# Pseudo-inverse steps, W and landmark scores on full 128x128 tiles of the multiplier, from batch 2 with block-diagonal operands

## The chip, the cores and the metric

The kernel runs on one core of one Trainium2 chip. The metric is the device time of one execution in microseconds (us); less is better. The matrix engine (PE) multiplies; VectorE (DVE), ScalarE (ACT) and GpSimd (POOL) work on elements; SyncE (SP) issues the transfers. PE can be used whole, as one array of 128x128, or as several smaller tiles that multiply side by side; the profile names the tile in each row (`128*128`, `128*64`, `32*32`: rows by columns).

## The reference, cut to what matters

Two stages for 8 batches of 576 positions: an approximate attention with 8 heads of 64 channels and 32 landmarks, then a layer with a Fourier transform and two large products. The attention:

```python
def _attn_ref(q, k, v):                       # (8, 8, 576, 64) each
    m, scale = 32, 1.0 / np.sqrt(D)
    q_lm = q.reshape(B, H, m, S // m, D).mean(axis=3)
    k_lm = k.reshape(B, H, m, S // m, D).mean(axis=3)
    A, Bm, C = sm(q, k_lm), sm(q_lm, k_lm), sm(q_lm, k)      # softmaxes
    Z = Bm.transpose(0, 1, 3, 2) / (norm1(Bm) * norminf(Bm) + 1e-06)
    for _ in range(6):
        Z = 2 * Z - Z @ Bm @ Z                # pseudo-inverse, 32x32 a head
    return A @ Z @ C @ v
def _moe_ref(x, w_ch1, w_ch2):                # x: (8, 576, 512)
    u = x + real(fft(fft(x, axis=1), axis=2))
    un = (u - mean(u)) / sqrt(var(u) + 1e-06)
    return u + relu(un @ w_ch1) @ w_ch2       # 512 to 2048 and back
```

## The kernel before, in words

**The order of the work.** Nothing is issued as the code runs. Each operation is recorded with its engine, a cost from a formula and what it reads and writes (`Order.op`, line 195; `Kernel.mm`, line 517, for multiplications). `Order.solve` (line 235) then plays the whole program with these costs and writes one fixed order for each engine: among what is ready it takes the lowest phase, and within a phase what has the longest chain behind it. Buffers come from pools (`SLOTS`, `BANKS`): four PSUM banks named `at` serve the attention, and from chunk 4 on two of these four are held for good by the second stage; `row` has six slots. On the chip, each engine runs its list strictly in that order. So a changed cost or a new operation can change the order on every engine. All instructions carry the line of the one place that emits them (L1307), so the rows are told apart by their tiles' names.

**The second stage** runs in 18 chunks of 256 positions. Each chunk multiplies by both weight matrices in three float16 products for each float32 one (`mm3`), with whole tiles: `hp<-unT,w` for the first matrix, `acc<-w,h`, `acc<-big,h`, `at<-big,h` and `at<-w,h` for the second. From chunk 4 (`SEVEN`) the second product is done in seven part products in place of eight, with sums made on DVE, ACT and POOL (`seven`).

**The attention** of the next batches is laid between these chunks. `attention` (line 658) loads q and k, makes the landmarks, and calls `landmarks` (line 923), which does the 32x32 work of all eight heads at once: heads are in two groups g of four, and the four 32x32 blocks of a group lie below each other on the 128 partitions. In order:

- landmark scores (lines 930 to 935): four multiplications `at<-lm,qbd` with 128x64 tiles, then a softmax to `Bd` and `nrm`.
- `BT` times its own transpose (lines 971 to 976): eight multiplications, one for each 32x32 block, `at<-BT` with 32x32 tiles.
- the values' product: `values` (batches 0 and 1) or `values_turned` (line 903, batches from `LATE` = 2 on) makes `R`, the product of the key softmax with v. In `values_turned` the 576 keys of a head go in four chunks of 128 keys and one of 64; the 64 left of two heads share the halves of one chunk, so this chunk is done in 64x32 tiles (first the low half, last the high half) and the others in 128x32 tiles. `load_v` (line 646) brings those 64 rows to both halves with two transfers.
- six pseudo-inverse steps (lines 982 to 995). `ES` holds the power E and the product S side by side, 64 columns for each group. A step multiplies each 32x32 block of E with its block of `ES`: eight multiplications `at<-nrm` or `at<-ES` in 32x32 tiles; the last one does only 32 columns. Then ACT copies E to the new `ES` and DVE adds to S.
- `nbd` (line 996): the result times a mask, as block-diagonal operands for what follows.
- W (lines 1002 to 1023): `at<-row,R` for the norm (two multiplications, 128x64 tiles) and `at<-R,row` (eight, 128x64 tiles).

A float32 multiplication is one instruction in the program and shows as two in the trace, each with a weight load; I call these passes.

Of the kernel before, what the change touches and what calls it, by code (L numbers as in the profile page):

```python
# [60 lines left out]
def tables():  # L61

    freqs = _tiles[0] + _tiles[1] + REST
    t1 = np.zeros((P, 4, 2, 160), np.float16)
    for i, (fn, o) in enumerate(((np.cos, 1), (np.sin, 0), (np.sin, 1), (np.cos, 0))):
        t1[:, i] = trig(fn, _tiles[0], freqs[o::2], S)
    t1t = np.zeros((P, 2, 2, 320), np.float16)
    t2 = np.zeros((P, 4, 2, 2, NC), np.float16)
    there = [f is not None for f in FREQS]
    for x, fn in enumerate((np.cos, np.sin)):  # L70
        t1t[:, x] = trig(fn, REST * 2, freqs[0::2] + freqs[1::2], S)
        for g in range(2):
# [4 lines left out]
    mask = np.zeros((P, 6), np.float32)  # L77
    mask[:, 0:4] = p[:, None] // 32 == np.arange(4)
    mask[:, 4:6] = p[:, None] // 64 == np.arange(2)
    diag = (p[:, None] % 32 == np.arange(32)).astype(np.float32)  # L80
    return t1, t1t, t2, diag, mask
# [5 lines left out]
KEEP = ("at", "row")  # L87
# [81 lines left out]
class Op:  # L169
    __slots__ = ("engine", "calls", "held", "took", "phase", "group", "margin", "seq", "before", "after", "tiles", "claims", "rank", "start", "end", "nbytes", "port", "name", "other", "urgent")  # L170


class Order:
# [21 lines left out]
    def op(self, engine, held, took, writes, reads, call, nbytes=0, port=False):  # L195
        o = self.bundle if engine == "PE" and self.bundle else None
        if o is None:
            o = Op()
            o.engine, o.calls, o.held, o.took, o.seq = engine, [], 0.0, 0.0, len(self.ops)
            o.phase, o.group, o.margin, o.nbytes, o.port = self.phase, self.group, self.margin, nbytes, port  # L200
            o.other, o.urgent = {}, False
            o.before, o.after, o.tiles, o.claims, o.name = dict.fromkeys(self.gate), [], {}, self.claims, ""
            self.claims = []
            self.ops.append(o)
            if engine == "PE" and self.bundle is not None:
                self.bundle = o
        o.calls.append(call)
        o.held += held
        o.took = o.held + took
        for v in reads:  # L210
            self.touch(o, v, False)
        for v in writes:
            self.touch(o, v, True)

# [20 lines left out]
    def solve(self):  # L235
# [11 lines left out]
        pipe, port, now, done = 0.0, 0.0, 0.0, []  # L247
# [58 lines left out]
        while events:  # L306
# [22 lines left out]
            for e in [e for e in best if e not in again] + again:  # L329
# [17 lines left out]
                o.start = now  # L347
                free[e] = now + o.held
# [72 lines left out]
class Kernel:  # L421
    def __init__(self, ctx, tc, NB, q, k, v, w1, w2, t1, t1t, t2, diag, mask, out):
# [20 lines left out]
        self.mask = self.const(mask, [P, 6], F32, "mask")  # L443
        self.mask4, self.mask2 = self.mask[:, 0:4], self.mask[:, 4:6]
# [72 lines left out]
    def mm(self, out, a, b, start=True, stop=True, share=1.0):  # L517
        n, m = math.prod(b.shape[1:]), math.prod(a.shape[1:])
        if a.dtype != F32:
            held = max(0.02, 0.003 + n / 2400 * share + (0.01 if share < 1.0 or 100 < n < 200 else 0.0))  # L520
        else:
            held = max(0.2, 0.02 + 4 * n / 2400) * (m / 128 if m < 128 else 1.0) * share
        self.order.op(
            "PE", held * self.cold, 0.2, [out], [a, b],
            (self.nc.tensor, "matmul", (out, a, b), {"start": start, "stop": stop, "skip_group_check": True}),
        )
        self.order.ops[-1].name = "mm"

    def tr(self, out, a, ident):
        self.order.op("PE", 0.21 * self.cold, 0.2, [out], [a, ident], (self.nc.tensor, "transpose", (out, a, ident), {}))  # L530
        self.order.ops[-1].name = "tr"

# [113 lines left out]
    def load_v(self, b, loads):  # L646
        for g in range(2):
# [182 lines left out]
    def values(self, loads, Cs, ci, R):  # L830
        V, A, mm, tr = self.V, self.A, self.mm, self.tr
        for g in range(2):
# [20 lines left out]
            V.tensor_scalar(R[:, g], ps[:, 0:64], Cs[g][1], ci[:, g : g + 1], ALU.mult, ALU.mult)  # L853
# [49 lines left out]
    def values_turned(self, loads, T, ci, R):  # L903
# [5 lines left out]
        low, high = slice(0, 64), slice(64, P)  # L909
        for g in range(2):  # L910
# [10 lines left out]
            V.tensor_scalar(R[:, g], ps[:, 0:64], ci[:, g : g + 1], 2.0**-14, ALU.mult, ALU.mult)  # L921

    def landmarks(self, b, loads, qbd, lm):
# [5 lines left out]
        R = small([P, 2, 64], "R")  # L929
# [6 lines left out]
        V.tensor_scalar(Bd.rearrange("p g m -> p (g m)"), ps[:, 0:64], 1.0 / 2592.0, None, ALU.mult)  # L936
# [33 lines left out]
        blocks = [slice(32 * i, 32 * i + 32) for i in range(4)]  # L970
        pse = self.at()
        self.together()
        for g in range(2):
            for i in blocks:
                mm(pse[i, 32 * g : 32 * g + 32], BT[i, g], BT[i, g])
        self.apart()
# [4 lines left out]
        ES = nrm[:, :, 0:2].rearrange("p g x m -> p g (x m)")  # L981
        for it in range(6):
            c0 = 0 if it < 5 else 32
            ps = self.at()
            self.together()
            for g in range(2):
                for i in blocks:
                    mm(ps[i, 64 * g + c0 : 64 * g + 64], ES[i, g, 0:32], ES[i, g, c0:])
            self.apart()
            pv = ps[:, 0:128].rearrange("p (g m) -> p g m", g=2)  # L990
            new = small([P, 2, 64], "ES", bufs=3)
            if it < 5:
                A.copy(new[:, :, 0:32], pv[:, :, 0:32])
            V.tensor_tensor(new[:, :, 32:64], ES[:, :, 32:64], pv[:, :, 32:64], ALU.add)
            ES = new
        nbd = self.row(512).rearrange("p (g i m) -> p g i m", g=2, i=4)
        for g in range(2):
            self.E.tensor_tensor(
                nbd[:, g].rearrange("p i (d m) -> p i d m", d=2), ES[:, g, 32:].unsqueeze(1).unsqueeze(1).broadcast_to([P, 4, 2, 32]),
                self.mask4.unsqueeze(2).unsqueeze(3).broadcast_to([P, 4, 2, 32]), ALU.mult,  # L1000
# [3 lines left out]
        for g in range(2):  # L1004
            mm(pst[64 * g : 64 * g + 64, 0:128], R[:, g], nbd[:, g, :, 0:32])
# [29 lines left out]
        def rest():  # L1035
            WC = [self.mid().bitcast(F16)[:, 0 : 4 * NC].rearrange("p (y x t) -> p y x t", y=2, x=2) for g in range(2)]
            for x in range(2):
# [3 lines left out]
                for ya, yb in ((0, 0), (0, 1), (1, 0)):  # L1041
                    for i in range(4):
                        at = 32 * (2 * (i % 2) + i // 2)
                        for g in range(2):
                            rows = slice(64 * g, 64 * g + 64)
                            mm(pss[g][at : at + 32, 0:NC], Wt[rows, ya, i], self.t2[rows, i, yb, x], yb == 0 and ya == 0, ya == 1, 0.125)
# [328 lines left out]
```

## Time and profile before

| what | value |
|---|---|
| median of 3 runs | 965.61 us (965.14 to 967.0) |
| the profiled execution's own time | 965.58 us |
| its span in the profile | 963.4 us |
| busy PE, PE weight loads | 911.0, 731.0 us |
| busy DVE, ACT, POOL | 760.1, 482.8, 216.5 us |
| PE instructions | 10510 |

The span is 2.2 us shorter than the execution's own time. In a group's row stand the line, the engine, the operation, the tiles written and read (buffer numbers left out), the shapes, the count, then the busy time in us and the mean of one in ns. In a timeline's row the first number is the start in us from the beginning of the span, the second the time from the first start to the last end of the merged instructions. Matmuls are pipelined: one that lasts 0.27 us in the profile can follow the one before after 0.11 us, so what a stretch costs PE is read from start to start.

### The profile page before, as it was taken

Reading aid. Unit: us, or ns where it says so; the run is one execution under the profiler, and the core shown is the slowest. Engines: PE = TensorE matmul, PEld = TensorE weight load, DVE = VectorE, ACT = ScalarE, POOL = GpSimd, SP = SyncE. Lnnn points to the kernel's source line nnn. Section 1 sums busy time; section 2 is a strip of 40 time slices with the busy share of each in tenths; the row PEclk is TensorE's granted clock in tenths of the full one; section 3 lists DMA queues with packets and bytes.
Section 4 is the critical chain, followed back from the end, with each engine's and each line's share of the span. In section 5 each row is a group of like instructions: output and inputs, shape, how many; then the busy total and the mean of one; then the engine's idle time right before and its main releaser. Section 6 shows DMA issues by size and latency. Waiting matters only on the chain. (4 is left out here: it accounts for less than half of the span.)

```text
span 963.4 us, 26055 instructions
## 1 busy us (share of the span) xinstructions
PE 911.0 (95%) x10510; PEld 731.0 (76%) x10510; DVE 760.1 (79%) x2016; ACT 482.8 (50%) x1007; POOL 216.5 (22%) x250
## 2 busy tenths in 40 slices
PE   5767999999999999999999999999999999999997
PEld 3546667666666788888887778887888878888886
DVE  7989996898898769887789886996698858665455
ACT  5999842355455445454454444545345533333332
POOL 0211210153643213321223002242031303101010
PEclk9768999999999999999999999999999999999999
DMA  9966110734737433556252733467235522435231
GB/s 350 355 226 178 41 37 13 182 105 95 258 90 189 157 89 104 155 124 213 67 155 88 195 104 89 133 130 216 67 100 154 132 74 73 120 112 117 82 105 50
DMA packets 161993, 128.23 MB, mean 133 GB/s; under 512 B 80080, under 2 KB 150736, under 8 KB 161744
## 3 DMA queue, kind: packets, MB, share of 16 engines
q1 hardware_dynamic: 161872, 126.57, 45.3%
q8 instruction: 82, 1.34, 0.6%
q14 instruction: 39, 0.32, 0.1%
HBM read 94.15 MB, written 14.68 MB: 113 GB/s over the span
## 5 line engine op out<-in xcount | busy, mean ns | idle before, releaser
L1307 PE MATMUL hp<-unT,w 128*128 128x256 f16 x3264 | 388.5, 273 | 10.3 <-DMA unT<-row 8.9
L1307 PEld LDWEIGHTS <-w 128*128 128x128 f16 (+1 forms) x3584 | 345.0, 99 | 68.5 <-issue 10.4
L1307 PEld LDWEIGHTS <-h 128*128 128x128 f16 x2604 | 247.2, 98 | 61.9 <-issue 6.6
L1307 PE MATMUL acc<-w,h 128*128 128x256 f16 (+1 forms) x1260 | 198.6, 294 | 1.1 <-DVE u L1307 0.4
L1307 DVE TENSOR_TENSOR sum<-ws 128x256 f32<-128x256 f32 (+1 forms) x278 | 99.8, 405 | 69.9 <-ACT ws L1307 68.1
L1307 ACT ACTIVATE ws<-hp 128x512 f32<-128x512 f32 x112 | 66.6, 595 | 140.1 <-PE hp L1307 139.9
L1307 ACT CAST h<-sum 128x640 f16<-128x640 f32 x112 | 81.1, 724 | 82.6 <-DVE sum L1307 68.1
L1307 PE MATMUL at<-big,h 128*128 128x256 f16 x672 | 110.1, 273 | 0.0
L1307 POOL TENSOR_TENSOR sum<-ws 128x256 f32<-128x256 f32 (+1 forms) x58 | 41.3, 727 | 252.9 <-ACT ws L1307 197.9
L1307 DVE TENSOR_TENSOR h<-sum,h 128x640 f16<-128x640 f32 x79 | 65.0, 823 | 19.2 <-ACT h L1307 18.0
L1307 POOL TENSOR_TENSOR h<-sum,h 128x640 f16<-128x640 f32 x33 | 46.4, 1405 | 150.3 <-ACT h L1307 150.3
L1307 ACT CAST row<-row 128x256 f16<-128x256 f32 (+1 forms) x76 | 36.7, 505 | 40.4 <-DVE row L1307 32.2
L1307 DVE TENSOR_REDUCE lm<-big 128x32 f32<-128x576 f32 (+1 forms) x48 | 44.3, 946 | 14.7 <-DMA big<-k_dram 8.1
L1307 PE MATMUL at<-w,h 128*128 128x256 f16 x336 | 55.0, 273 | 0.0
L1307 PE MATMUL acc<-big,h 128*128 128x256 f16 x336 | 55.0, 273 | 0.0
L1307 PEld LDWEIGHTS <-big 128*128 128x128 f16 (+1 forms) x768 | 40.8, 104 | 11.0 <-issue 5.0
L1307 ACT CAST h<-ws 128x256 f16<-128x256 f32 x112 | 45.3, 404 | 2.7
L1307 DVE SCALAR_TENSOR_TENSOR u<-at,scw,row 128x128 f32<-128x128 f32 (+3 forms) x120 | 39.0, 386 | 3.7 <-PE at L1307 3.5
L1307 DVE TENSOR_TENSOR h<-ws,h 128x256 f16<-128x256 f32 x95 | 40.5, 426 | 0.0
L1307 ACT ACTIVATE big<-big 128x1168 f16<-128x1168 f32 (+1 forms) x26 | 25.3, 983 | 29.2 <-DMA big<-q_dram 21.7
L1307 PEld LDWEIGHTS <-mt 64*128 64x128 f16 (+1 forms) x752 | 28.6, 98 | 14.5 <-issue 8.0
L1307 DVE SCALAR_TENSOR_TENSOR u<-acc,winv,u 128x512 f32<-128x512 f32 x50 | 35.3, 741 | 3.0 <-PE acc L1307 2.7
(223 smaller groups left out, 1254.7 us busy)
## 6 DMA issues: line engine op xcount, KB each, us to landing
big<-sums SPq DMA_DIRECT2D x336, 128.0 KB, 2.2
w<-w_dram SPq DMA_DIRECT2D x22, 512.0 KB, 8.1
big<-q_dram SPq DMA_DIRECT2D x16, 584.0 KB, 6.2
big<-k_dram SPq DMA_DIRECT2D x16, 576.0 KB, 4.8
out_dram<-u SPq DMA_DIRECT2D x36, 256.0 KB, 2.2
big<-v_dram SPq DMA_DIRECT2D x12, 512.0 KB, 4.8
big<-w_dram SPq DMA_DIRECT2D x10, 512.0 KB, 6.5
sums<-row SPq DMA_DIRECT2D x40, 128.0 KB, 2.5
```

The lines of the kernel that those rows point to most:

```text
L1307: getattr(engine, name)(*map(real, args), **{k: real(x) for k, x in kw.items()})
```

## The change

**Block-diagonal operands.** From batch 2 on, the product of `BT` and the six steps use whole 128x128 tiles: the left operand of each group is spread to a block-diagonal 128x128 matrix in a `row` buffer (the 32 columns times a mask, four times beside each other), and one multiplication for each group replaces four. For the product of `BT` and the first step the spreading is given to DVE or POOL, as the planner decides; in the five following steps it reads the PSUM result and so is DVE's. ACT's copy stays.

**W and scores**, in all batches: `R` becomes a kept buffer `Rz` of [128, 2, 128] whose other half is zero (cleared once by POOL), so that `at<-Rz,row` is two multiplications with 128 columns that add into one bank; the eight of `at<-R,row` become four with 128 columns each; the order of heads in `nbd` and `Wt` goes along. The landmark scores are two multiplications with 128 columns in place of four with 64; half of their result isn't used, and two DVE operations take the other half in place of one.

**The values' product**, from batch 2: the fifth chunk is multiplied whole, with zero rows of v standing against the other head's keys, all in 128x32 tiles; 20 multiplications a group as before. `load_v` brings that chunk with three transfers in place of two.

**The planner's costs**: the least cost of a whole float32 multiplication goes from 0.2 to 0.13 us, and each change of the tile shape between multiplications costs 0.12 us (`SWITCH`).

```diff
-        self.mask = self.const(mask, [P, 6], F32, "mask")
+        self.mask = self.const(mask, [P, 10], F32, "mask")
+        self.Rz = self.kept([P, 2, P], F32, "Rz")
+        self.G.memset(self.Rz, 0.0)
...
-            held = max(0.2, 0.02 + 4 * n / 2400) * (m / 128 if m < 128 else 1.0) * share
+            held = max(0.032, max(0.13, 0.02 + 4 * n / 2400) * (m / 128 if m < 128 else 1.0) * share)
...
+                if o.modes:
+                    if o.modes[0] != mode:
+                        o.held += SWITCH
+                        o.took += SWITCH
+                    mode = o.modes[-1]
...
-                for x in range(2):
-                    self.dma(to[64 * x : 64 * x + 64, 4], src[0:64, 4])
+                of = lambda t, x: t[:, 4].rearrange("p (r x d) -> p r x d", r=2, x=2)[:, :, x]
+                self.dma(of(to, 0), of(src, 0))
+                for half in range(2):
+                    self.dma(of(to, 1)[64 * half : 64 * half + 64], of(src, 1)[64 - 64 * half : 128 - 64 * half])
...
-            tiles = [(0, low, 4, 4)] + [(x, slice(0, P), 5 * x + c, c) for c in range(4) for x in range(2)] + [(1, high, 4, 4)]
-            for x, rows, blk, c in tiles:
-                for r in range(2):
-                    i, at = 2 * r + x, 64 * g + 32 * r
-                    mm(ps[32 * i : 32 * i + 32, 0:64], E[rows, blk, at : at + 32], vf[rows, c, 64 * i : 64 * i + 64],
-                       (x, c) in ((0, 4), (1, 0)), (x, c) in ((0, 3), (1, 4)))
+            for c in range(5):
+                for i in range(4):
+                    at = 64 * g + 32 * (i // 2)
+                    blk = c if c == 4 else 5 * (i % 2) + c
+                    mm(ps[32 * i : 32 * i + 32, 0:64], E[:, blk, at : at + 32], vf[:, c, 64 * i : 64 * i + 64], c == 0, c == 4)
...
-            for pr in range(2):
-                mm(ps[64 * pr : 64 * pr + 64, 32 * g : 32 * g + 32], qbd[:, 2 * g + pr], lm[:, g, 64 + 32 * pr : 96 + 32 * pr])
+            mm(ps[:, 64 * g : 64 * g + 64], flat(qbd[:, 2 * g : 2 * g + 2]), lm[:, g, 64:128])
...
+        full = b >= LATE
+        def diagonal(src, E):
+            t = self.row(256).rearrange("p (g i m) -> p g i m", g=2, i=4)
+            for g in range(2):
+                E.tensor_tensor(
+                    t[:, g], src(g).unsqueeze(1).broadcast_to([P, 4, 32]), self.mask4.unsqueeze(2).broadcast_to([P, 4, 32]), ALU.mult
+                )
+            return t
+        def blockwise(ps, lhs, rhs, n, c0=0):
...
+                if full:
+                    mm(ps[:, out], lhs[:, g].rearrange("p i m -> p (i m)"), rhs[:, g, c0:])
+                else:
+                    for i in blocks:
+                        mm(ps[i, out], lhs[i, g], rhs[i, g, c0:])
...
+        lhs = diagonal(lambda g: nrm[:, g, 0], self.E) if full else ES[:, :, 0:32]
         for it in range(6):
...
-                for i in blocks:
-                    mm(ps[i, 64 * g + c0 : 64 * g + 64], ES[i, g, 0:32], ES[i, g, c0:])
+            blockwise(ps, lhs, ES, 64, c0)
             if it < 5:
                 A.copy(new[:, :, 0:32], pv[:, :, 0:32])
+                lhs = diagonal(lambda g: pv[:, g, 0:32], V) if full else new[:, :, 0:32]
...
-            mm(pst[64 * g : 64 * g + 64, 0:128], R[:, g], nbd[:, g, :, 0:32])
+            mm(pst[:, 0:128], R[:, g], nbd[:, g, :, 0:32], g == 0, g == 1)
...
-            for i in range(4):
-                at = 64 * (2 * g + i % 2)
-                w = R[:, g].rearrange("p (m o) -> p o m", o=2)
-                mm(ps[64 * (i // 2) : 64 * (i // 2) + 64, at : at + 64], nbd[:, g, i],
-                   w[:, ::-1] if i % 2 else w)
+            for pair in range(2):
+                at = 64 * (2 * g + pair)
+                w = R[:, g, 64 * g : 64 * g + 64].rearrange("p (m o) -> p o m", o=2)
+                mm(ps[:, at : at + 64], flat(nbd[:, g, 2 * pair : 2 * pair + 2]), w[:, ::-1] if pair else w)
```

What this does to the order is seen at two places. The first is PE's list in batch 5, at a pseudo-inverse step in the middle of the second stage's stream (`h` and `w` belong to that stage, `kbd` to the attention's scores). Before:

```order
L1307 LDWEIGHTS big_65
L1307 MATMUL at_105<-kbd_134,big_65 128x2x32
L1307 MATMUL at_102<-ES_164 32x64 x8
L1307 LDWEIGHTS h_96
L1307 MATMUL acc_108<-w_111,h_96 128x256
```

and in the changed kernel, at the same step:

```order
L1345 LDWEIGHTS h_96
L1345 MATMUL at_103<-big_69,h_96 128x256
L1345 MATMUL at_105<-ES_163,row_80 128x64 x2
L1345 LDWEIGHTS h_96
L1345 MATMUL at_104<-w_111,h_96 128x256
```

Eight multiplications of 32 rows have become two of 128 rows, whose left operand is now the `row` buffer; what stands around the step is another part of the stream.

The second place is DVE's list in the same batch, from one step's operations to the next one's (`sum` and `h` are the second stage's, `mt`, `amx` and `asum` the attention's softmax). Before:

```order
L1307 TENSOR_TENSOR ES_163<-nrm_145,at_102 128x2x32
L1307 TENSOR_TENSOR sum_100<-ws_99 128x256
L1307 TENSOR_REDUCE amx_175<-at_105 128x16
L1307 TENSOR_TENSOR sum_100<-ws_99 128x128
L1307 TENSOR_TENSOR h_95<-ws_99,h_95 128x256
L1307 TENSOR_TENSOR mt_77<-at_105,amx_175 128x512
L1307 TENSOR_REDUCE asum_177<-mt_77 128x16
L1307 TENSOR_SCALAR asum_177<-asum_177 128x16
L1307 RECIPROCAL asum_177<-asum_177 128x16
L1307 TENSOR_TENSOR mt_77<-mt_77,asum_177 128x512
L1307 TENSOR_TENSOR ES_164<-ES_163,at_102 128x2x32
```

and in the changed kernel:

```order
L1345 TENSOR_TENSOR row_80<-at_102,mask 128x128 x2
L1345 TENSOR_TENSOR ES_163<-ES_162,at_102 128x2x32
L1345 TENSOR_TENSOR sum_100<-ws_98 128x256
L1345 TENSOR_TENSOR sum_100<-ws_98 128x128
L1345 TENSOR_TENSOR h_94<-ws_98,h_94 128x256
L1345 TENSOR_TENSOR row_81<-row_83,row_81 128x512
L1345 TENSOR_TENSOR h_94<-sum_100,h_94 128x640
L1345 TENSOR_TENSOR sum_101<-ws_99 128x256 x2
L1345 TENSOR_TENSOR row_79<-at_105,mask 128x128 x2
L1345 TENSOR_TENSOR ES_164<-ES_163,at_105 128x2x32
```

Each step has two more DVE operations of 128x128 ahead of its addition, between the second stage's own operations.

More of the change, by code (lines that the diff above doesn't have):

```diff
@@ L86 @@
 IN_ORDER = ("u", "big", "ml", "mt", "unT", "h", "ws", "sum", "hp", "acc")
-KEEP = ("at", "row")
+KEEP, SWITCH = ("at", "row"), 0.12
 LINK, PATIENCE = 0.05, 0.0
@@ L169 @@
 class Op:
-    __slots__ = ("engine", "calls", "held", "took", "phase", "group", "margin", "seq", "before", "after", "tiles", "claims", "rank", "start", "end", "nbytes", "port", "name", "other", "urgent")
+    __slots__ = ("engine", "calls", "held", "took", "phase", "group", "margin", "seq", "before", "after", "tiles", "claims", "rank", "start", "end", "nbytes", "port", "name", "other", "urgent", "modes")
 class Order:
@@ L213, in op, with mode @@
             self.touch(o, v, True)
+    def mode(self, mode):
+        o = self.ops[-1]
+        if o.modes and o.modes[-1] != mode:
+            o.held += SWITCH
+            o.took += SWITCH
+        o.modes.append(mode)
     def touch(self, o, v, write):
@@ L526, in mm @@
         )
+        size = lambda v: 128 if v > 64 else 64 if v > 32 else 32
+        self.order.mode((size(a.ap.ap[0][1]), size(m)))
         self.order.ops[-1].name = "mm"
@@ L928, in landmarks @@
         Bd = small([P, 2, 32], "Bd")
-        R = small([P, 2, 64], "R")
+        R = self.Rz
         ps = self.at()
@@ L932, in landmarks @@
         for g in range(2):
-            for pr in range(2):
-                mm(ps[64 * pr : 64 * pr + 64, 32 * g : 32 * g + 32], qbd[:, 2 * g + pr], lm[:, g, 64 + 32 * pr : 96 + 32 * pr])
+            mm(ps[:, 64 * g : 64 * g + 64], flat(qbd[:, 2 * g : 2 * g + 2]), lm[:, g, 64:128])
         self.apart()
-        V.tensor_scalar(Bd.rearrange("p g m -> p (g m)"), ps[:, 0:64], 1.0 / 2592.0, None, ALU.mult)
+        for pr in range(2):
+            rows = slice(64 * pr, 64 * pr + 64)
+            V.tensor_scalar(
+                Bd[rows], ps[rows, 0:128].rearrange("p (g r m) -> p g r m", g=2, r=2)[:, :, pr], 1.0 / 2592.0, None, ALU.mult
+            )
         mx = small(2, "bmx")
@@ L970, in landmarks @@
         blocks = [slice(32 * i, 32 * i + 32) for i in range(4)]
-        pse = self.at()
-        self.together()
-        for g in range(2):
-            for i in blocks:
-                mm(pse[i, 32 * g : 32 * g + 32], BT[i, g], BT[i, g])
-        self.apart()
+        full = b >= LATE
[4 more added lines that the diff above has]
+                    t[:, g], src(g).unsqueeze(1).broadcast_to([P, 4, 32]), self.mask4.unsqueeze(2).broadcast_to([P, 4, 32]), ALU.mult
+                )
+            return t
+        def blockwise(ps, lhs, rhs, n, c0=0):
+            self.together()
+            for g in range(2):
+                out = slice(n * g + c0, n * g + n)
+                if full:
[3 more added lines that the diff above has]
+                        mm(ps[i, out], lhs[i, g], rhs[i, g, c0:])
+            self.apart()
+        pse = self.at()
+        blockwise(pse, diagonal(lambda g: BT[:, g], self.E) if full else BT, BT, 32)
         for g in range(2):
@@ L1041, in rest @@
                 for ya, yb in ((0, 0), (0, 1), (1, 0)):
-                    for i in range(4):
-                        at = 32 * (2 * (i % 2) + i // 2)
+                    for k, i in enumerate((0, 2, 1, 3)):
+                        at = 32 * k
                         for g in range(2):
                             rows = slice(64 * g, 64 * g + 64)
-                            mm(pss[g][at : at + 32, 0:NC], Wt[rows, ya, i], self.t2[rows, i, yb, x], yb == 0 and ya == 0, ya == 1, 0.125)
+                            mm(pss[g][at : at + 32, 0:NC], Wt[rows, ya, k], self.t2[rows, i, yb, x], yb == 0 and ya == 0, ya == 1, 0.125)
                 self.apart()
```

23 lines of the change are left out of this document (11 added, 12 removed).

## The prediction

> **What bounds the kernel now.** I read the page's busy times and slices first, then the windows, to see which engine is full and where.
>
> ```profile
> PE 911.0 (95%) x10510; PEld 731.0 (76%) x10510; DVE 760.1 (79%) x2016; ACT 482.8 (50%) x1007; POOL 216.5 (22%) x250
> PE   5767999999999999999999999999999999999997
> PEclk9768999999999999999999999999999999999999
> ...
> 150.00:830.00 680.00, 669.18 (x7980) 537.40 (x7978) 555.87 (x1484) 320.73 (x688) 182.25 (x207) 1.00 0.46 128
> ```
>
> PE is busy in nine tenths or more of every slice but the first six and the last, at the full granted clock (9s, and 1.00 in the window). The windows' row gives, after the stretch and its length, the busy time of PE, weight loads, DVE, ACT and POOL: from 150 to 830 us, where batches 2 to 7 of the attention lie between chunks of the second stage, PE lacks 680.00 - 669.18 = 10.8 us, and DVE is busy in 555.87 / 680 = 82%. After 830 us only the second stage is left. So the end is set by how long PE's list takes, and a us less of work on it is a us less at the end, as long as nothing makes PE wait more. What waiting there is comes from DVE, in this row of the waits (time in total, times, longest):
>
> ```profile
> PE at L1307 <- DVE big L1307: 4.9, 4, 2.7
> ```
>
> Now what the changed pieces cost on PE. The duration of a matmul is pipelined, so I read from start to start in the timeline. A pseudo-inverse step of 64 columns, and the last one of 32:
>
> ```profile
> 758.35 0.49 PE L1307 MATMUL at<-big,h 128*128 128x256 f16 x3
> 758.68 0.49 PE L1307 MATMUL at<-w,h 128*128 128x256 f16 x3
> 759.10 0.42 PE L1307 MATMUL at<-ES 32*32 32x64 f32 x16
> 759.46 0.50 PE L1307 MATMUL at<-big,h 128*128 128x256 f16 x3
> ...
> 410.31 0.49 PE L1307 MATMUL at<-w,h 128*128 128x256 f16 x3
> 410.74 0.33 PE L1307 MATMUL at<-ES 32*32 32x32 f32 x16
> 410.99 0.50 PE L1307 MATMUL at<-big,h 128*128 128x256 f16 x3
> ```
>
> Three of the stream's matmuls take 758.68 - 758.35 = 0.33 us, 0.11 each. From 758.68 to 759.46 are 0.78 us, of which 0.33 belong to the three; the step costs PE 0.45. The last one costs 410.99 - 410.31 - 0.33 = 0.35. Its 16 passes run as 4 rounds of 4 tiles; 32 columns fewer save 0.10, so 64 columns in 4 rounds are 0.20, and the other 0.25 of a step is what entering and leaving the small tiles costs: 759.10 stands 0.09 later than the stream would have gone on, and the rest lies at the exit.
>
> **The change part by part.** First W and the scores, in the same way:
>
> ```profile
> 341.31 0.49 PE L1307 MATMUL acc<-big,h 128*128 128x256 f16 x3
> 341.73 0.42 PE L1307 MATMUL at<-lm,qbd 128*64 128x32 f32 x8
> 342.08 0.50 PE L1307 MATMUL at<-big,h 128*128 128x256 f16 x3
> ...
> 436.81 0.60 PE L1307 MATMUL hp<-unT,w 128*128 128x256 f16 x4
> 437.34 0.44 PE L1307 MATMUL at<-row,R 128*64 128x128 f32 x4
> 437.71 0.94 PE L1307 MATMUL hp<-unT,w 128*128 128x256 f16 x7
> ...
> 440.81 1.15 PE L1307 MATMUL hp<-unT,w 128*128 128x256 f16 x9
> 441.89 0.74 PE L1307 MATMUL at<-R,row 128*64 128x64 f32 x16
> 442.56 0.83 PE L1307 MATMUL acc<-w,h 128*128 128x256 f16 x6
> ```
>
> Scores: 0.77 - 0.33 = 0.44. The norm's product: 0.90 - 4 x 0.11 = 0.46. W: 1.75 - 9 x 0.109 = 0.77.
>
> After the change these are whole-tile float32 passes with 32 to 128 columns. The trace has such passes, without a change of tile around them, with 128 columns and with 4:
>
> ```profile
> 714.34 1.15 PE L1307 MATMUL hp<-unT,w 128*128 128x256 f16 x9
> 715.32 0.39 PE L1307 MATMUL at<-nrm,ones_bd 128*128 128x128 f32 x2
> 715.55 0.82 PE L1307 MATMUL acc<-w,h 128*128 128x256 f16 x6
> ...
> 718.17 0.49 PE L1307 MATMUL at<-big,h 128*128 128x256 f16 x3
> 718.49 0.28 PE L1307 MATMUL at<-amax,ones 128*128 128x4 f32 x2
> 718.64 0.49 PE L1307 MATMUL at<-w,h 128*128 128x256 f16 x3
> ...
> L1307 PEld LDWEIGHTS <-h 128*128 128x128 f16 x2604 | 247.2, 98 | 61.9 <-issue 6.6 <-ACT h L1307 1.3 <-DVE h L1307 1.3
> L1307 PEld LDWEIGHTS at<-nrm,ones_bd 128*128 128x128 f32 x16 | 2.7, 205 | 0.5 <-DVE nrm L1307 0.2
> ```
>
> Two passes of 128 columns cost 715.55 - 714.34 - 9 x 0.109 = 0.23, so 0.11 each. Two passes of 4 columns still cost 718.64 - 718.17 - 0.33 = 0.14. If only the columns counted, they would cost next to nothing. What fits both is the load of the 128x128 float32 operand: 0.11 us, the first one hidden behind the matmul before it, each later one not hidden by a pass shorter than itself. The last two rows point the same way (205 ns for such a load against 98 for a float16 one). So n passes cost (n - 1) x 0.11 and the last pass's own columns: 0.03 for up to 32, 0.06 for 64 (half of 128's 0.11), 0.11 for 128.
>
> The Trainium skill, "TensorE: Matmul & The Clock Gate", section "LDWEIGHTS (loading the stationary operand)", has a load take its columns divided by 1.2 GHz, whatever the rows, and its section on weight-path modes excludes float32 from the fast load. An estimate by that page: 107 ns for 128 columns, so a whole-tile step costs 3 x 0.107 + 0.06 = 0.38. It speaks against this change, and the two passes of 4 columns agree with it.
>
> By the rows, then, four passes of 64 columns cost 0.39, of 32 columns 0.36, of 128 columns 0.44, and eight of 64 columns 0.83. For each of batches 2 to 7: scores 0.44 - 0.39 = 0.05; the first step and the four after it, 5 x (0.45 - 0.39) = 0.30; the last step and the product of `BT` (32 columns as well, the same 16 passes) 2 x (0.35 - 0.36) = -0.02; the norm's product 0.46 - 0.44 = 0.02; W 0.77 - 0.83 = -0.06. Together 0.29, in six batches 1.7 us. In batches 0 and 1 only scores, norm and W change: 0.01, nothing.
>
> The values' product loses its inner tile changes:
>
> ```profile
> 552.19 0.49 PE L1307 MATMUL acc<-big,h 128*128 128x256 f16 x3
> 552.62 1.12 PE L1307 MATMUL at<-big,big 64*32 64x64 f32 x40
> 553.67 0.50 PE L1307 MATMUL at<-big,h 128*128 128x256 f16 x3
> ...
> 431.33 0.49 PE L1307 MATMUL at<-big,h 128*128 128x256 f16 x3
> 431.75 1.95 PE L1307 MATMUL at<-big,big 64*32 64x64 f32 x80
> 433.64 1.16 PE L1307 MATMUL acc<-w,h 128*128 128x256 f16 x9
> ...
> 126.13 0.90 PE L1307 MATMUL at<-big,ml 128*32 128x64 f32 x40
> 126.96 1.47 PE L1307 MATMUL acc<-w,h 128*128 128x512 f16 x6
> ```
>
> One group costs 553.67 - 552.19 - 0.33 = 1.15 with two inner changes (64x32, 128x32, 64x32). Batch 1 has the form without the split low and high halves, with one inner change at its end: 126.96 - 126.13 = 0.83, and 0.09 for the entry, 0.92. So one change is at most 1.15 - 0.92 = 0.23, and the new form, with none, costs between 0.69 and 0.92; I take the middle, 0.80. Two groups back to back cost 433.64 - 431.33 - 0.33 = 1.98 before and 2 x 0.80 - 0.25 = 1.35 after. Before and after, four batches have them back to back and two apart: 4 x 0.63 + 4 x 0.35 = 3.9 us (2.5 to 5.2 between the ends).
>
> PE's list thus gets 1.7 + 3.9 = 5.6 us shorter (4.2 to 6.9).
>
> What is added elsewhere: ten spreadings of PSUM results a batch on DVE, and four from SBUF, of which the planner gave 7 of 24 to POOL: 77 on DVE. The nearest row is a DVE operation of the same size with one operand in PSUM and one repeated:
>
> ```profile
> L1307 DVE TENSOR_TENSOR ae<-at,amx 128x128 f32<-128x128 f32 x8 | 2.3, 284 | 0.1
> ```
>
> 77 x 0.284 = 22 us, which brings DVE from 82 to (555.9 + 22) / (680 - 5.6) = 86%. PE's stream covers them; if it doesn't, what waits behind them in DVE's list is the stage's `sum` and `h`, and for these PE's next `acc` matmuls. The row above shows that PE does wait for DVE at times. At worst PE's 10.8 us grow as DVE's free share shrinks, by 18 / 14, that is by 3.1; at best nothing. I take 1.4, since most steps have work of PE to spare. The third transfer for v's last chunk and its smaller rows, the clearing of `Rz` and the second DVE operation on the scores (8 in all) cost nothing: SP issues v's loads well ahead, and POOL is busy in 22%. If v's chunk came late, the values' product of a batch would wait for it.
>
> The sum, against the profiled execution's own time, which is the median to 0.03 us: 965.6 - 5.6 + 1.4 = 961.4 us.
>
> **The rivals.** *The loads don't bind.* If the exposed 0.11 after the 4-column passes were a cost paid once for leaving float32, four passes of 64 columns would be 0.24, of 32 columns 0.12, and W 0.48: scores save 0.20, five steps 1.05, the two of 32 columns 0.46, norm 0.02, W 0.29, together 2.0 a batch and 12 us in six, 0.5 in the first two. With 3.9 from the values and 1.4 of waits: 965.6 - 16.4 + 1.4 = 950.6. For it speaks that no row here shows a whole-tile float32 pass of 64 columns; against it that passes of 128 columns show no such cost. A tenth.
>
> *The waits eat the gain.* The planner writes a new order everywhere, from costs that know nothing of the chip's drift; PE's 10.8 us of waiting is low, and a new order finds more easily 16 than 5. If it grows by about 5.6 us, the time is 965.6. For it speaks a DVE at 86%, against it that the waits of before are few and that attention is far ahead of its users.
>
> *Slower: the steps' chain.* A step's result used to be ready for the next one after one ACT copy; now it waits for two DVE operations in DVE's own order, 2 x 0.284 = 0.57 us, and holds one of the two `at` banks left so long. If PE reaches each of the 36 multiplications before its operand is there and stands for 0.57, that is 20.5 us: 965.6 - 5.6 + 20.5 = 980.5. It decides from (5.6 + 1.9) / 36 = 0.21 us of standing a step. Against it: in the changed order some 3 us or more of PE's work stand between two steps of one batch, three times what matmul, spreading and handover need.
>
> **How the numbers follow.** A measurement of this kernel can tell about 0.2%, 1.9 us, from no change. Forecast 0.64, loads that don't bind 0.10, eaten gain 0.17, slower 0.09. The forecast lies between 965.6 - 6.9 = 958.7 and 965.6 - 4.2 + 3.1 = 964.5 by its bounds, and a new order can move it further by some us either way. The range, 952 to 967, leaves out the first and the last rival. Faster: 0.64 + 0.10 = 0.74; the same 0.17; slower 0.09.
>
> **What would show it.** In the profile after: a whole-tile step should stand in the stream for 0.39 us (0.24 if the loads don't bind), its passes about 0.11 apart; the values' product for about 0.8, W for 0.83; DVE's new rows 0.28 each. PE's waiting from 150 us to the attention's end should be 11 to 14 us. I am wrong if steps cost 0.25 or less, if PE's waits for DVE grow by more than 5 us, or if the sum of PE's list didn't shrink by 4 to 7 us.

## The result, and the profile after

| | kernel before | changed kernel |
|---|---|---|
| median | 965.38 us (964.02 to 967.0, 4 runs) | 972.71 us (971.84 to 974.42, 4 runs) |
| the profiled execution, its span | 965.58, 963.4 us | 971.84, 970.1 us |

The ratio is 1.0077, 95% interval 1.0056 to 1.0099: slower by 0.8%, clear of noise, where I had forecast 961.4. The page of the changed kernel, busy times and slices:

```profile
PE 910.4 (94%) x9910; PEld 745.8 (77%) x9910; DVE 780.1 (80%) x2101; ACT 484.4 (50%) x1007; POOL 222.9 (23%) x258
PE   4766999999999999999999989999999999999997
PEclk9777999999999999999999999999999999999999
```

The bound is the same engine at the same clock. But PE has 600 instructions fewer and is as long busy, and its first slices are thinner. Where the second stage begins and ends shows in the first and last start of `hp<-unT,w`, before and then after (shortest, median and longest duration in ns, first and last start in us):

```profile
L1307 PE MATMUL hp<-unT,w x3264: 269/273/421, 77.2 to 952.3; 128*128 128x256 f16 x192
```

```profile
L1345 PE MATMUL hp<-unT,w x3264: 269/273/422, 81.3 to 959.2; 128*128 128x256 f16 x192
```

The last start is 6.9 us later. Of that, 4.1 are there before the first chunk begins, a stretch that my sum had no term for; the other 2.8 come between, where I had forecast -5.6 + 1.4 = -4.2. Windows of the changed kernel (the attention's last multiplications, `at<-Wx,mt`, start at 856.2 us here and at 847.7 before, so it was not over by 830 us, as I had written; PE lacks nothing there in either kernel):

```profile
150.00:830.00 680.00, 664.15 (x7373) 546.54 (x7371) 571.21 (x1550) 319.49 (x683) 189.85 (x216) 1.00 0.46 126
830.00:844.00 14.00, 14.00 (x131) 12.54 (x129) 8.07 (x23) 6.08 (x11) 0.66 (x1) 1.00 0.36 95
```

PE lacks 680.00 - 664.15 = 15.85 us where it lacked 10.8, and I had said 11 to 14. Its waits from 85 us on, the longest four rows of 17.2 us in all (before: 12.7):

```profile
PE at L1345 <- DVE big L1345: 5.3, 4, 3.1
PE at L1345 <- DVE u L1345: 2.4, 4, 1.0
PE at L1345 <- DVE Rz L1345: 2.1, 2, 1.3
PE at L1345 <- ACT big L1345: 1.3, 2, 0.8
```

The first of these is as long as before (4.9); the other three were next to nothing before (`u` 0.3, the others not in the list). None of them names a spreading of a step; they are small waits at many places. And the changed pieces, from start to start as in the prediction:

```profile
772.74 1.47 PE L1345 MATMUL hp<-unT,w 128*128 128x256 f16 x12
774.05 0.56 PE L1345 MATMUL at<-ES,row 128*128 128x64 f32 x4
774.45 0.49 PE L1345 MATMUL acc<-w,h 128*128 128x256 f16 x3
...
428.50 0.49 PE L1345 MATMUL acc<-big,h 128*128 128x256 f16 x3
428.83 0.53 PE L1345 MATMUL at<-ES,row 128*128 128x32 f32 x4
429.19 0.49 PE L1345 MATMUL at<-big,h 128*128 128x256 f16 x3
...
439.67 0.49 PE L1345 MATMUL at<-big,h 128*128 128x256 f16 x3
440.10 1.32 PE L1345 MATMUL at<-big,big 128*32 128x64 f32 x80
441.35 0.83 PE L1345 MATMUL acc<-w,h 128*128 128x256 f16 x6
...
339.20 0.81 PE L1345 MATMUL acc<-w,h 128*128 128x256 f16 x6
339.85 1.00 PE L1345 MATMUL at<-Rz,row 128*128 128x64 f32 x8
340.70 0.49 PE L1345 MATMUL acc<-w,h 128*128 128x256 f16 x3
```

A step costs 774.45 - 772.74 - 12 x 0.109 = 0.40 (forecast 0.39), one of 32 columns 0.69 - 0.33 = 0.36 (0.36), the values' product of two groups 1.68 - 0.33 = 1.35 (1.35), W 1.50 - 0.65 = 0.85 (0.83). The groups that stand alone waited in this profile; in the run e2_old_costs below, with the same instructions, one group stands free in the stream and costs 1.11 - 0.33 = 0.78 (0.80):

```profile
791.40 0.49 PE L1345 MATMUL acc<-big,h 128*128 128x256 f16 x3
791.82 0.77 PE L1345 MATMUL at<-big,big 128*32 128x64 f32 x40
792.51 0.50 PE L1345 MATMUL at<-big,h 128*128 128x256 f16 x3
```

So the pieces did shrink as forecast. At the cost that each has where nothing holds it up, 30 steps give 1.7 us, the scores 0.3, the 12 products of 32 columns -0.2, W -0.5, the values 3.9: in six batches PE's list is 5.4 us shorter. From the first chunk on the time is 2.8 longer all the same, so what went into waiting grew by the difference, about 8.2 us: -5.4 + 8.2 + 4.1 at the start are the 6.9. This 8.2 is a remainder, which takes in whatever else the new order changed in PE's list, and not read from rows: the profile's idle time shows 5 of it (15.85 against 10.8). A matmul that lasts 0.27 us and could follow after 0.11 leaves no idle time in the profile when it is up to 0.16 late, which would hide such waits. (The expectations below put the waiting before at 22 us, counted from the distances between starts; such a count moves by several us with what is taken as the usual distance.)

### The profile page after: what moved, and what is told of

It reads as the page before. It is cut to its first block, busy times and chain, and to the rows that moved or that the text cites. A ratio compares the mean times of both kernels' runs of the same rounds, so it can differ in the third digit from the quotient of the medians.

```text
span 970.1 us, 24978 instructions
## 1 busy us (share of the span) xinstructions
PE 910.4 (94%) x9910; PEld 745.8 (77%) x9910; DVE 780.1 (80%) x2101; ACT 484.4 (50%) x1007; POOL 222.9 (23%) x258
## 4 chain that ended last, share of the span: by engine, by line
PE 63%; DVE 18%; ACT 9%; DMA 6%; issue 3%; SPq 1%; POOL 0%; DVEq 0%; ACTq 0%; POOLq 0%
PE hp L1345 27%; PE at L1345 19%; PE acc L1345 16%; DVE u L1345 3%; DMA big<-big 2%; DVE row L1345 2%; DVE sum L1345 2%; ACT w L1345 2%; ACT big L1345 2%; DMA big<-q_dram 2%; ACT h L1345 2%; DVE mt L1345 1%; DVE big L1345 1%; ACT ws L1345 1%; DVE h L1345 1%
## 5 line engine op out<-in xcount | busy, mean ns | idle before, releaser
L1345 PEld LDWEIGHTS <-h 128*128 128x128 f16 x2604 | 249.9, 99 | 62.6 <-issue 8.4
L1345 DVE TENSOR_TENSOR sum<-ws 128x256 f32<-128x256 f32 (+1 forms) x277 | 104.8, 423 | 66.5 <-ACT ws L1345 66.0
L1345 POOL TENSOR_TENSOR h<-sum,h 128x640 f16<-128x640 f32 x31 | 43.6, 1406 | 97.7 <-ACT h L1345 97.3
```

Source lines behind the costliest of these rows:

```text
L1345: getattr(engine, name)(*map(real, args), **{k: real(x) for k, x in kw.items()})
```

## The experiments

All compare with the kernel before on the same chip. The theories, as the expectations name them: **A**, the new order costs the time (narrow: the planner's new costs are at fault; wide: the order of before is a lucky one); **B**, the added work on DVE costs it (later **B1**, its time, and **B2**, ACT standing for it); **C**, the whole-tile scores and W cost it at the slow clock of the first batches (before, the granted clock is 0.81 from 20 to 40 us and 0.70 from 40 to 90).

**e1_costs**: the kernel before with the planner's new costs alone, the same instructions.

```diff
-            held = max(0.2, 0.02 + 4 * n / 2400) * (m / 128 if m < 128 else 1.0) * share
+            held = max(0.032, max(0.13, 0.02 + 4 * n / 2400) * (m / 128 if m < 128 else 1.0) * share)
...
+        self.order.mode((size(a.ap.ap[0][1]), size(m)))
```

> The kernel before with the planner's new costs alone (least cost of a whole float32 multiplication 0.13, 0.12 for each change of tile shape); no instruction is other, only their order. Theory A (the new order costs it: the planner's changed costs lay everything out anew, and the time comes back as waits of PE and a later first chunk): 968 to 977 us, PE's list as long as before. Theory B (the work added on DVE costs it): 964 to 967 us, as before, since no DVE work is added. Theory C (whole-tile W and scores in the slow-clocked first batch cost it): as before too, 964 to 967 us, first chunk at 77 us.

979.73 us, ratio 1.0152 (1.0128 to 1.0175). Without any new instruction, the order that these costs lead to is slower by twice what the whole change is. PE lacks 16.6 us between 150 and 850 us, where it lacked 10.8.

**e2_old_costs**: the changed kernel with the old costs.

```diff
-KEEP, SWITCH = ("at", "row"), 0.12
+KEEP, SWITCH = ("at", "row"), 0.0
...
-            held = max(0.032, max(0.13, 0.02 + 4 * n / 2400) * (m / 128 if m < 128 else 1.0) * share)
+            held = max(0.2, 0.02 + 4 * n / 2400) * (m / 128 if m < 128 else 1.0) * share
```

> All of the change's instructions with the planner's costs of before (0.2 at least, nothing for a change of tile shape). Theory A in its narrow form (the new costs are to blame): 958 to 963 us. Theory A in its wide form (any new order is worse than the one before, whatever its costs): 966 to 975 us, with waits spread over other places. Theory B (DVE's added work): 970 to 975 us, as the changed kernel. Theory C: first chunk again some 4 us later than before, 965 to 969 us.

968.86 us, 1.0047 (1.0031 to 1.0064); the first chunk starts at 79.7 us. Somewhat under half of the loss goes; the gain that A's narrow form promised (958 to 963) doesn't come. PE still lacks 13.0 us between 150 and 850 us.

**e3_values**: the kernel before with the values' product and its loads alone (the diff's parts in `load_v` and `values_turned`, of which the core stands here); its order stays but for a few places on each engine.

```diff
-            tiles = [(0, low, 4, 4)] + [(x, slice(0, P), 5 * x + c, c) for c in range(4) for x in range(2)] + [(1, high, 4, 4)]
...
+            for c in range(5):
+                for i in range(4):
+                    at = 64 * g + 32 * (i // 2)
+                    blk = c if c == 4 else 5 * (i % 2) + c
+                    mm(ps[32 * i : 32 * i + 32, 0:64], E[:, blk, at : at + 32], vf[:, c, 64 * i : 64 * i + 64], c == 0, c == 4)
```

> The kernel before with the new values' product and its three loads alone; the planner's costs of these are the same as before, so the order stays all but the same. If PE's list sets the end, as the prediction says, 3.9 us less: 960.5 to 963 us. If the time taken out of PE's list comes back as waiting elsewhere: 964 to 967 us.

964.18 us, 0.9994 (0.9974 to 1.0013). From the first to the last start of `hp<-unT,w` pass 871.9 us, 3.2 less than before (forecast 3.9), with as much idle time (11.05 us between 150 and 850), but the first chunk starts 0.9 later. The profiled span is 960.9, 2.5 less; the median is 0.6 less, and the interval ends at 2.5 less. Even a pure saving on PE's list shows only in part.

**e4_link** and **e8_mask**: the kernel before with an edit that changes nothing but the planner's arithmetic.

```diff
-LINK, PATIENCE = 0.05, 0.0
+LINK, PATIENCE = 0.06, 0.0
```

```diff
-    mask = np.zeros((P, 6), np.float32)
+    mask = np.zeros((P, 10), np.float32)
```

> The kernel before with one number of the planner moved that no instruction depends on (the time it adds for a handover, 0.05 to 0.06): the same instructions in another order. It measures what another order is worth by itself. Theory A wide: 3 to 10 us off 965.4, more likely slower, by waits of PE and the time of the first chunk. Theories B and C: within 2 us of 965.4.

> The kernel before with one edit that does nothing on the chip to speak of: the table of masks gets four more columns that nobody reads, as in the change. In the planner's reckoning its load is 6 ns longer, and from there on the planner writes another order on every engine. By the wide form of A (the order of before is a good draw, any other costs some us) the time is 966 to 975. If only the new costs make bad orders (A narrow), it is that of before within 2 us.

971.93 us, 1.008 (1.0063 to 1.0098), for the first, with its first chunk at 81.8 us as in the changed kernel; 964.69 us, 0.9994 (0.9981 to 1.0007), for the second. So an order alone can cost 7 us, but the order of before is no rare one: the second is another on every engine and as good. A in its wide form, that any other order costs some us, falls here.

**e5_same_order**: all of the change's instructions in the order of before. The planner is made to reckon the new operations at nothing and places them when they fall due.

```diff
+                    if o.quiet:
+                        o.start = o.end = now
+                        done.append(o)
...
+            self.order.quiet = True
             for g in range(2):
                 E.tensor_tensor(
                     t[g], src(g).unsqueeze(1).broadcast_to([P, 4, 32]), self.mask4.unsqueeze(2).broadcast_to([P, 4, 32]), ALU.mult
                 )
+            self.order.quiet = False
```

**e6_spreads** and **e7_steps** are the kernel before, in its own order, with the 84 spreadings alone, unread, and with the steps and the product of `BT` alone:

```diff
+        if b >= LATE:
+            diagonal(lambda g: BT[:, g])
...
-                for i in blocks:
-                    mm(ps[i, 64 * g + c0 : 64 * g + 64], ES[i, g, 0:32], ES[i, g, c0:])
+            blockwise(ps, lhs, ES, 64, c0)
```

To make room for the spreadings' own buffers, these three runs and the two that follow from them (e9, e10) also keep fewer small buffers: `ES` two in place of three, `Bd` one in place of two. The order of all other operations in the traces is that of before on every engine.

> All of the change's instructions, laid into the order of before: DVE, ACT, POOL and SP have the lists of before with the 84 spreadings, the second DVE operation on the scores and the third load put in where they fall due (the spreadings all on DVE, in buffers of their own), and the planner's old costs. If the change lost its time by the new order (A), PE's list is 5.6 to 6.3 us shorter, its first chunk starts at 77 to 78.5 us as before, its waits stay within 3 us of before's 22, and the time is 958 to 962 us. If the added work on DVE costs it (B), PE's waits grow by 8 us or more and the time is 966 or above. If the whole-tile scores and W at the slow clock at the start cost it (C), the first chunk starts at 80 us or later and the time is 961 to 965.

> The kernel before, in its own order and with its own multiplications, and beside them the 84 spreadings on DVE (6 batches x 7 x 2), whose results nobody reads: the added DVE work alone. By A, and by the prediction's term, PE's waits grow by 0 to 3 us, most likely 1.4, and the time is that of before + 0 to 3. By B they cost 7 us or more: 972.

> The kernel before, in its own order, with the product of BT and the six steps on whole tiles from batch 2 (their operands spread on DVE), and nothing else. The prediction's terms: five steps save 0.30 a batch, the two products of 32 columns lose 0.02, so 1.7 us less of PE's list in six batches, and 1.4 us more waiting for DVE: 965 us, no change that can be told. By the rival of the steps' chain 0.57 us of standing at each of 36 multiplications: 984. By B as in the run with the spreadings alone.

978.54 us, 1.0144 (1.0122 to 1.0166); 973.18, 1.0086 (1.0069 to 1.0102); 975.96, 1.012 (1.0096 to 1.0143). I had expected 958 to 962 from the first. What I had expected under B came: the order of before is good only for the work that it was written for. In it, 24 us more on DVE that it doesn't reckon with cost 8 us, though DVE has a fifth of its time free; how much of the 8 is due to the fewer buffers, no run tells. The waits of e6_spreads showed a second suspect: ACT stands behind the spreading that reads the same PSUM bank, 20 times.

```profile
ACT ES L1342 <- DVE spread L1342: 29.6, 20, 4.3
```

**e9_spreads_behind** and **e10_order_behind** put the spreadings behind ACT's copy (in e6_spreads and e5_same_order).

```diff
                 A.copy(new[:, :, 0:32], pv[:, :, 0:32])
+                copied = self.order.ops[-1]
...
+                if after:
+                    self.order.ops[-1].before[after] = None
```

> As e6_spreads (the kernel before with 84 unread spreadings on DVE), but the spreadings of a step stand behind ACT's copy of the same PSUM result, and not ahead of it: in e6_spreads the trace shows ACT standing 29.6 us at its copies for the spreading on the same bank, where before it didn't stand for DVE. If that standing of ACT is what cost e6_spreads its 8 us (B2), the time is within 2.5 us of before: 965 to 967.5. If DVE's 24 us of work cost it (B1), it stays 971 or above.

> As e5_same_order (all instructions of the change in the order of before), with the spreadings of a step behind ACT's copy of the same bank. PE's list is some 4 to 5 us shorter than before's. By B2 the waits that e5_same_order had over before's, 19 us, are mostly gone, and the time is 960 to 966. By B1, or if it is the longer way from one step to the next (copy, two spreadings, sum), it stays 972 or above.

972.86 us, 1.0083 (1.006 to 1.0106), and 975.52, 1.0092 (1.0067 to 1.0117). In e9_spreads_behind DVE waits for ACT instead, and hardly:

```profile
ACT ES L1345 <- PE at L1345: 14.9, 10, 5.1
DVE spread L1345 <- ACT ES L1345: 1.2, 3, 0.7
```

Between e6_spreads and e9_spreads_behind nothing changes: the 29.6 us of ACT's standing cost nothing that can be told there. Between e5_same_order and e10_order_behind the ratio falls from 1.0144 to 1.0092, so there the standing did cost some 3 to 5 us (3.0 between the medians, 0.5% between the ratios). B2 falls as the main cause, since 8 us or more are left in both; B1 stands for an order that doesn't know of the work. The Trainium skill, "PSUM — Partial Sum Buffer", section "PSUM bank collisions raise a hardware error", wants any two engines kept apart on the same bank and the same 32 partitions, readers too; the two runs agree (first ACT waits for DVE's read, then DVE for ACT's).

**e11_no_spreads**: the changed kernel in exactly its own order, without the spreadings.

```diff
-            (self.nc.tensor, "matmul", (out, a, b), {"start": start, "stop": stop, "skip_group_check": True}),
+            (self.nc.tensor, "matmul", (out, a if lhs is None else lhs, b), {"start": start, "stop": stop, "skip_group_check": True}),
...
+                o.calls = []
```

> The changed kernel with exactly its own order on every engine, but the 84 spreadings left out: the steps and the product of BT multiply by the identity in their place, so the pseudo-inverse isn't computed. If the spreadings (their time on DVE, ACT's standing at the same bank, the way from step to step) cost the changed kernel its gain (B), the time falls by 6 us or more, to 966 or below. If the new order by itself does (A), it stays within 2.5 us of 972.7, since the order is the same, and the first chunk starts at 81 us in either case.

973.35 us, 1.0087 (1.0067 to 1.0107): no faster than the changed kernel. In the window of 150 to 850 us PE lacks 15.85 us in the changed kernel and 12.8 here, and the first chunk starts at 81.3 us in both (the changed kernel's row first):

```profile
150.00:850.00 700.00, 684.15 (x7556) 564.45 (x7554) 584.74 (x1583) 328.24 (x697) 191.91 (x218) 1.00 0.46 126
150.00:850.00 700.00, 687.24 (x7561) 567.44 (x7559) 574.22 (x1507) 327.73 (x697) 188.85 (x211) 1.00 0.46 126
```

In the order that was planned with them, doing the spreadings costs no time that can be told (the interval is some 2 us wide to each side); their share of PE's idle time, 3 us, is about the most that my term allowed. So the spreadings' time on DVE isn't what the changed kernel lost (B falls), and what it lost is in the order. That order was planned with room for the spreadings, so the run doesn't say what planning for them costs.

**e12_after_link** and three pairs of further orders: the changed kernel with `LINK` at 0.06, and both kernels with 0.04, 0.055 and 0.07, the same edit as in e4_link:

```diff
-LINK, PATIENCE = 0.05, 0.0
+LINK, PATIENCE = 0.04, 0.0
```

> The changed kernel, with one constant of the planner at 0.06 and not 0.05, as e4_link was for the kernel before: the same instructions in another order. If the order that the change got is a bad draw (A), another one lies lower, 960 to 969, as likely as not; if the added instructions cost it (B), it stays at 970 or above. The first chunk, 81.3 us in the changed kernel, may move by 2 to 4 us.

> The kernel before with the planner's constant LINK at 0.04: the same instructions in another order. If the spread of orders is what decides (A), somewhere in 963 to 974, and the first chunk starts at 77 to 82 us; in the planner's own reckoning it starts 0.6 us earlier than in the kernel before. If before's instructions are easy to order (the change makes a harder plan), within 2 us of 965.

> The changed kernel with LINK at 0.04: its instructions in another order. By A it lies on the average of the three pairs 4 to 6 us below the kernel before with the same constant (PE's list is 5 us shorter), each pair with some 4 us of luck either way. If the change makes a harder plan, it lies 3 us or more above its partner in all three pairs.

> The kernel before with LINK at 0.055. By A in 963 to 974; the planner's reckoning has the first chunk 2.6 us later than in the kernel before, so 967 or above is likelier. By the other theory within 2 us of 965.

> The changed kernel with LINK at 0.055. By A 958 to 970, and the mean of the three pairs 4 to 6 us below; by the other theory 3 us or more above its partner. The planner's reckoning has the first chunk at the same time as in the changed kernel, so I expect it near 81 us.

> The kernel before with LINK at 0.07. By A in 963 to 974; the planner's reckoning has the first chunk 1.6 us later than in the kernel before. By the other theory (before's instructions are easy to order) within 2 us of 965.

> The changed kernel with LINK at 0.07. The planner's reckoning has the first chunk 2.9 us later than in the changed kernel, so that this pair is the worst for it: by A 964 to 976; by the other theory 3 us or more above its partner.

| `LINK` | before, us | changed, us | difference | first chunk before, changed |
|---|---|---|---|---|
| 0.04 | 963.75 | 977.66 | +13.9 | 76.7, 81.8 |
| 0.05 | 965.38 | 972.71 | +7.3 | 77.2, 81.3 |
| 0.055 | 969.06 | 973.23 | +4.2 | 79.9, 80.0 |
| 0.06 | 971.93 | 966.62 | -5.3 | 81.8, 79.3 |
| 0.07 | 963.8 | 983.01 | +19.2 | 78.5, 83.6 |

I had expected the changed kernel 4 to 6 us below on the average of the three new pairs; it lies above in all three, by 4.2 us or more, as the other theory (the change makes a harder plan) said, and 983.01 lies above the 964 to 976 that A allowed. Over the five pairs the mean is +7.9, close to the 7.3 of the change itself, but the differences run from -5.3 to +19.2, so its size is loose. The windows of the two ends, before and changed with 0.04:

```profile
150.00:850.00 700.00, 692.57 (x8221) 558.22 (x8219) 570.70 (x1514) 327.89 (x701) 199.15 (x224) 1.00 0.46 128
```

```profile
150.00:850.00 700.00, 682.39 (x7518) 560.72 (x7517) 580.65 (x1580) 326.73 (x697) 191.21 (x214) 1.00 0.46 125
```

PE lacks 7.4 us and 17.6. From the same window of all: before 10.8, 11.7, 6.2, 7.4, 9.4, 7.9 (e8_mask third), changed 15.85, 12.5, 17.6, 16.2, 16.6. The two sets don't meet. So the changed kernel's orders are worse as a rule, by some 7 us of idle time here and 2.5 us at the start (means of the first chunk's start: 78.7 over the six, 81.2 over the five); its 966.62 is its lucky draw, and even that isn't faster than the kernel before (ratio 1.0021, 1.0004 to 1.0038).

## Why the prediction was wrong

*PE's list.* Right, in the pieces and in the sum: 5.4 us shorter where I said 5.6 (4.2 to 6.9). The 0.80 for one group of the values, a middle between two bounds, came out at 0.78 to 0.80, which is luck in part. The loads of the float32 operands do bind: 0.40 for a step and not 0.24, so that rival falls. The estimate that the prediction set beside it from the Trainium skill, "TensorE: Matmul & The Clock Gate", section "LDWEIGHTS (loading the stationary operand)", was 0.38, and the trace agrees.

*"A us less of work on it is a us less at the end, as long as nothing makes PE wait more."* This is the step that failed, by its condition. I gave PE's waiting one term, DVE's added work, 1.4 us with 3.1 at most. DVE's part was about that: PE's idle time falls by 3 us when the spreadings are taken out, and DVE's new rows last what I took (282 ns for 284):

```profile
L1345 DVE TENSOR_TENSOR row<-at,mask 128x128 f32<-128x128 f32 x60 | 15.1, 282 | 7.3 <-PE at L1345 3.5 <-ACT ES L1345 3.1 <-DMA unT<-row 0.5
```

What I had no term for is the new order itself, which I had named only as a rival and let end where it cancels the gain, at 965.6. Its price: 4.1 us at the start, of which about 1 isn't the order's (below), and about 8.2 us of waiting in place of 1.4, together 10.9 us more than my sum. The 0.09 that I gave to a slower kernel was for another mechanism, the steps' chain.

*The start.* I read the windows from 150 us on and took the stretch before it for unchanged, though the slices showed PE less than nine tenths busy there (the first four, not six as I wrote). Rows of the first batch, before and after:

```profile
11.90 0.59 PE L1307 MATMUL at<-lm,qbd 128*64 128x32 f32 x8
12.42 0.59 PE L1307 MATMUL at<-amax,ones 128*128 128x4 f32 x2
...
14.01 0.49 ACT L1307 ACTIVATE ml<-at,cb 128x288 f32<-128x288 f32 x1
...
14.48 2.20 ACT L1307 ACTIVATE big<-big,sc 128x1024 f16<-128x1024 f32 x2
```

```profile
12.11 1.12 PE L1345 MATMUL at<-lm,qbd 128*128 128x64 f32 x4
...
13.02 0.53 PE L1345 MATMUL at<-amax,ones 128*128 128x4 f32 x2
...
14.96 2.20 ACT L1345 ACTIVATE big<-big,sc 128x1024 f16<-128x1024 f32 x2
...
17.54 0.48 ACT L1345 ACTIVATE ml<-at,cb 128x288 f32<-128x288 f32 x1
```

Two things are seen: the scores take 0.91 us and not 0.52 to the next matmul, and ACT's second exponential stands behind the 2.20 us of `big`, where it stood ahead. The first of them is part of C. Why whole-tile passes are so slow here is open: they stand 0.21 us apart at 12 us and 0.11 at 100 us, but the windows show a granted clock of 1.00 from 0 to 30 us in both kernels. W of the first batch, at 36 to 42 us, does stand where the granted clock is low (0.63 from 30 to 81 us before, 0.66 from 30 to 85 after); its passes last 1.95 us together, 1.18 before. How much the start owes to all this can be told: it is at 79.1 and 78.8 us with the change's instructions in the order of before (e5_same_order, e10_order_behind), and at 77.2 to 78.1 in the five profiles of that order without the whole-tile scores and W (before, e3, e6, e7, e9). So about 1 us of the 4.1, by single profiles; the rest is the order's, since the start moves between 76.7 and 81.8 us for the kernel before by the order alone.

*The steps' chain.* Not it: PE stood hardly at all before the steps' multiplications, and not for a spreading.

```profile
L1345 PE MATMUL at<-ES,row 128*128 128x64 f32 x96 | 13.8, 267 | 1.1 <-ACT big L1345 0.8 <-ACT hl L1345 0.3
```

*What makes the changed kernel's orders worse* is shown only in part. The new costs do it by themselves to the instructions of before: 979.73 lies 7.8 us above the slowest of six orders written with the old costs. The changed instructions with the old costs took 968.86, within those six (963.75 to 971.93) and below the mean of the changed kernel's five, 974.6. Each is a single draw, and draws of one kind differ by 8 to 16 us. The idle time between 150 and 850 us speaks for the instructions too: 13.0 us with the changed instructions and the old costs, above all six of the kernel before (6.2 to 11.7). So how the loss is shared between costs and instructions stays open. One suspect that no run tests: the new cost of a whole float32 multiplication, 0.13 us, fits the passes of 4 columns (0.14 for two), but a step of two with 64 columns takes 0.40 and the four of W 0.85, so that the planner reckons 0.26 and 0.52 where the old 0.2 gave 0.40 and 0.80. Another: the spreadings take `row` buffers and hold an `at` bank longer, and the planner has to plan round that. No run says whether the changed instructions under the old costs would on the average beat the kernel before. No kernel here was faster than it: the lowest, 963.75 us with `LINK` at 0.04, has the ratio 0.9986 (0.9968 to 1.0003).

## What to carry to other kernels

Where a planner writes the whole order, an edit's price is the price of its pieces plus that of a new draw, and the draw can be the larger: a planner's constant without any work to it moved this kernel by 7 us, and other costs of the same instructions by 15. Draw several orders of both kernels, with a constant that means nothing, before a gain of half a per cent is believed or given up. Change costs in a planner apart from the instructions, and read the stretch before the steady part too.

## What the runs showed that I had not expected

- The transfer of four more columns of the mask table, 2 KB, is reckoned 6 ns longer by the planner, and from there every engine has another order; the kernel took the same time (964.69 against 965.0).
- Work added to an order that doesn't know of it cost a third of its length (24 us on DVE, 8 us, with somewhat fewer buffers); the same work taken out of an order that does know of it gave back nothing that can be told (973.35 against 972.71). So the free fifth of DVE's time says little on what an addition costs.
- ACT can stand 29.6 us more at no cost that can be told: e6_spreads and e9_spreads_behind differ by 0.3 us. It isn't so everywhere: e5_same_order, where it stood 31.8 us, got 3 us faster when the spreadings went behind ACT's copy (e10_order_behind).
